# First group of an attention and softplus-layer kernel: keys pooled by TensorE, softplus ahead of weight conversions

## The chip, the cores and the metric

The kernel runs on one core of a Trainium2 chip. Its engines work side by side, each through its own list of instructions in a fixed order: TensorE (PE; weight loads are shown as PEld), VectorE (DVE), ScalarE (ACT), GpSimd (POOL), and SyncE (SP), which here only issues DMAs. The metric is the device time of one execution in microseconds (us), less is better.

## The reference

```python
# attention, 64 heads (8 batches x 8), 576 tokens, 64 wide; keys and values pooled by 8
k_p = k.reshape(B, H, 72, 8, D).mean(axis=3)
v_p = v.reshape(B, H, 72, 8, D).mean(axis=3)
scores = 1/8 * q @ k_p^T
scores -= max(scores); attn = exp(scores); attn /= sum(attn) + 1e-9
x = (attn @ v_p)                       # as 4608 tokens x 512
# softplus layer, 512 -> 2048 -> 512
h = x @ w_in
g = max(h, 0) + log1p(exp(-abs(h)))
x = g @ w_out
# gated experts: a skip score and 8 gate logits for each token, one expert of 8 (512 -> 1024 -> 512)
```

## The kernel before

The tokens go through attention and the softplus layer in nine groups of 512. A group's attention is four *units*, one for each pair of heads; the four units of group g+1 are made while group g is in the softplus layer. Group 0 has no such cover: its four units (`unit0`) run first, with on-chip room that later holds weights.

A unit pools the keys, copies the pooled keys of two heads into a block-diagonal tile `kbd` (two copies on ACT), multiplies (`s`), takes maximum, difference, exponential, sum and reciprocal (`shares`), transposes the shares (on TensorE in group 0, by DVE and 12 DMAs later), pools and transposes v into `vp`, and multiplies again (`o`). Every product that needs full precision is done with a high and a low half: `xh` is `o` rounded (ACT), `xl` the rest (DVE). Unit 3 of a group writes the last quarter of `xh` and `xl`.

The softplus layer runs in 16 chunks of 128 hidden columns. `p1(g, c)` has 12 matmuls into a bank `h`; four quarters of the input, three matmuls each. The softplus is Abs, Exp, Ln on ACT (L718 to L720), the sum `a` on DVE (L721), the rounded half `gh` on ACT (L723), the rest `gl` on DVE (L725). There are two banks `h`, and L721 reads a bank last, so p1 of a chunk waits for L721 of the chunk two before. `p2(g, c)` adds 12 matmuls into four banks `y`, two chunks behind p1. When the last chunk of a group is through, `finish` copies the four banks to `rows` (ACT, L113) and makes 36 gating products of 128x512 with them on DVE (L119).

The weights of this layer arrive as pairs of 32-bit words that hold both halves of the bits, and have to be converted during group 0 (`load_weights`): two unpacks on ACT (`unpack`), two joins on DVE (`join`), the rounded half on ACT, the rest on DVE. The first four 128-row blocks go in halves of 512 columns, six of them ahead of group 0 through three buffers `raw`, the others in pairs of whole blocks of 1024 columns. Each of these steps is one turn of a generator, and the loops that make group 0 call it between chunks (`weights(n)`); `ready(c)` says how many turns chunk c needs.

The order of the instructions on each engine is made when the kernel is built: the code emits them in the order of its loops, and a scheduler moves them by its own estimate of when each could run. In the trace the rows of each engine come in the order so made, so an instruction that waits holds up those behind it on its engine.

Of the kernel before, what the change touches and what calls it, by code (L numbers as in the profile page):

```python
# [9 lines left out]
F32 = mybir.dt.float32  # L10
F32R = mybir.dt.float32r
BF16 = mybir.dt.bfloat16
I32 = mybir.dt.int32
# [7 lines left out]
P = 128  # L21
# [8 lines left out]
XW = 520  # L30
BIG = float(1 << 20)
LAG = 2


@with_exitstack
def tile_kernel(ctx, tc, qT, kT, vT, wbits, w9, w1, w2, out):
# [383 lines left out]
    with ExitStack() as ph:  # L420
# [6 lines left out]
        ep = ph.enter_context(tc.tile_pool(name="ep", bufs=1))  # L427
        ps_a = ph.enter_context(tc.tile_pool(name="ps_a", bufs=2, space=PSUM))
        ps_h = ph.enter_context(tc.tile_pool(name="ps_h", bufs=2, space=PSUM))
        ps_y = ph.enter_context(tc.tile_pool(name="ps_y", bufs=1, space=PSUM))  # L430

        kbd = []
        for i in range(2):
# [21 lines left out]
            return pool.tile([P, n], F32, tag=tag, name=tag)  # L455

        EARLY = 4
        STEPS = 6 * EARLY + 6 * (8 - EARLY // 2)
# [4 lines left out]
        def load_weights():  # L463


            bits = wbits.bitcast(I32)

            def unpack(lo, hi):
                nc.scalar.activation(out=hi.bitcast(F32), in_=hi.bitcast(F32), func=AF.Copy,
                                     scale=2.0 ** -112)  # L470
                nc.scalar.activation(out=lo, in_=lo.bitcast(U32), func=AF.Copy, scale=7.49 * 2.0 ** -32)

            def join(v, lo, hi):
                nc.vector.scalar_tensor_tensor(out=v, in0=hi, scalar=3, in1=lo,
                                               op0=ALU.logical_shift_left, op1=ALU.bitwise_or)
# [3 lines left out]
            def half(c, j, first):  # L479
                wh, wl = (wt[c // 2][:, c % 2, i, j * 512:(j + 1) * 512] for i in range(2))  # L480
                if first:
                    raw = room("raw", 1024, True).bitcast(I32).rearrange("p (a b) -> p a b", b=2)
                else:
                    raw = scratch.tile([P, 512, 2], I32, tag="raw", name="raw")
                nc.sync.dma_start(out=raw.rearrange("p a b -> p (a b)"),
                                  in_=bits[c * P:(c + 1) * P, j * 1024:(j + 1) * 1024])
                lo, hi = raw[:, :, 0], raw[:, :, 1]
                unpack(lo, hi)
# [10 lines left out]
            for c in range(EARLY):  # L499
                for j in range(2 if c >= LAG else 1):  # L500
                    yield from half(c, j, True)
            for i in range(EARLY // 2, 8):
                raw = wtile(i, f"raw{i}", 2, 1024, 2, dtype=I32)
                for j in range(2):
                    c = 2 * i + j
                    nc.sync.dma_start(out=raw[:, j].rearrange("p a b -> p (a b)"), in_=bits[c * P:(c + 1) * P, :])
                vs = []
                for j in range(2):
                    lo, hi = raw[:, j, :, 0], raw[:, j, :, 1]
                    unpack(lo, hi)  # L510
                    yield
                    v = scratch.tile([P, 1024], I32, tag="raw", name="v")
                    join(v, lo, hi)
                    vs.append(v.bitcast(F32))
                    yield
                wt.append(wtile(i, f"wt{i}", 2, 2, 1024, dtype=F32R))
                for j in range(2):
                    wh, wl = wt[i][:, j, 0], wt[i][:, j, 1]
                    nc.scalar.activation(out=wh, in_=vs[j], func=AF.Copy)
                    nc.vector.tensor_tensor(out=wl, in0=vs[j], in1=wh.bitcast(F32), op=ALU.subtract)  # L520
                    yield
            for c in range(LAG):
                yield from half(c, 1, False)

        pooled = {}
        count = [0]
        def keys(u, k, kv):
            if u not in pooled:
                kp = pp.tile([P, SP], F32, tag="kp", name="kp")
                nc.vector.tensor_reduce(kp, k.rearrange("p (s w) -> p s w", w=8), AX.X, ALU.add)  # L530
                v = kv()
                nc.sync.dma_start(out=v, in_=vT[u])
                pooled[u] = (kp, v, None)
            kp = pooled[u][0]
# [4 lines left out]
            return kb  # L539

        def shares(e, sm, rc):
            nc.scalar.activation(out=e, in_=e, func=AF.Exp, scale=1.0 / 64)
# [32 lines left out]
        def unit0(hp, us, xh, xl):  # L575
# [3 lines left out]
            nc.sync.dma_start(out=q, in_=qT[u, :, r0:r0 + rn])  # L579
            yield  # L580
            yield
            banks = [ps_y.tile([P, 512], F32, tag=f"y{hp % 2 * 2 + i}", name="s") for i in range(2)]
            kb = keys(u, k, lambda: room("kv", 576, True))
            for t in range(T):
                nc.tensor.matmul(banks[t // 3][:, t % 3 * 144:(t % 3 + 1) * 144],
                                 lhsT=q[:, t * P:(t + 1) * P], rhs=kb, start=True, stop=True)
# [3 lines left out]
            for b, (i, j) in enumerate(((0, 3), (3, 4))):  # L590
                s3 = banks[b][:, :(j - i) * 144].rearrange("p (a k) -> p a k", k=SP)
                m = mx[:, 2 * i:2 * j]
                nc.vector.tensor_reduce(m, s3, AX.X, ALU.max)
                nc.vector.tensor_tensor(out=e[:, 2 * i:2 * j], in0=s3, op=ALU.subtract,
                                        in1=m.unsqueeze(2).to_broadcast([P, 2 * (j - i), SP]))
            shares(e, sm, rc)
            yield
            yield
            kp, v, _ = pooled[u]
            v8 = v.rearrange("p (s w) -> p w s", w=8)  # L600
            pv = ps_h.tile([P, 512], F32, tag="h", name="pv")
            for w in range(8):
                nc.tensor.matmul(pv[:SP, :P], lhsT=v8[:, w], rhs=ident, start=w == 0, stop=w == 7)
# [103 lines left out]
        def p1(g, c):  # L707
# [9 lines left out]
            a = ap.tile([P, G], F32, tag="a", name="a")  # L717
            nc.scalar.activation(out=a, in_=h, func=AF.Abs)  # L718
            nc.scalar.activation(out=a, in_=a, func=AF.Exp, scale=-1.0)
            nc.scalar.activation(out=a, in_=a, func=AF.Ln, bias=1.0)  # L720
            nc.vector.scalar_tensor_tensor(out=a, in0=h, scalar=0.0, in1=a, op0=ALU.max, op1=ALU.add)  # L721
            gh = gp.tile([P, G], F32R, tag="gh", name="gh")
            nc.scalar.activation(out=gh, in_=a, func=AF.Copy)  # L723
            gl = gp.tile([P, G], F32R, tag="gl", name="gl")
            nc.vector.tensor_tensor(out=gl, in0=a, in1=gh.bitcast(F32), op=ALU.subtract)  # L725
            return gh, gl

        def p2(g, c, gh, gl):
# [13 lines left out]

        def ready(c):
            if c < EARLY:
                return 3 * (2 * c - min(c, LAG)) + 3
            return 3 * (2 * EARLY - LAG) + 6 * ((c - EARLY) // 2) + 6
# [264 lines left out]
```

## Time and profile before

| | us |
|---|---|
| median of 3 runs (lowest to highest) | 1370.47 (1370.27 to 1371.11) |
| profiled execution | 1378.22 |
| its span, first to last instruction | 1376.5 |
| TensorE busy | 1338.4 (97%) |
| VectorE busy | 847.6 (62%) |
| ScalarE busy | 594.6 (43%) |
| GpSimd busy | 309.6 (22%) |
| mean granted TensorE clock | 0.994 of full |

TensorE is busy nearly throughout, and shares over the whole span say little of the first 150 us, where the other engines have their fullest stretch. Windows of the span, the order in time of single engines and the list of waits show that part.

### The profile page before, as it was taken

The numbers are of one execution on the slowest core, as the hardware profiler recorded it, in microseconds if no ns is written. First come the engines' busy times: TensorE is split into PE (matmuls) and PEld (weight loads), VectorE is DVE, ScalarE is ACT, GpSimd is POOL, SyncE is SP. The second block draws the span as 40 slices with busy tenths as digits, with TensorE's granted clock in tenths as the row PEclk, the third lists the DMA queues.
The fourth block names the chain that finished last, engine by engine and source line by source line (L and its number), as shares of the span: only waits on it lengthen the run. The fifth ranks groups of instructions, "written<-read, shape, count | busy, mean of one in ns | idle before, by whom it ended". The sixth has DMA issues, their size and how long they took to land. (4 is left out here: it accounts for less than half of the span.)

```text
span 1376.5 us, 21364 instructions
## 1 busy us (share of the span) xinstructions
PE 1338.4 (97%) x7030; PEld 1114.9 (81%) x7030; DVE 847.6 (62%) x1951; ACT 594.6 (43%) x1076; POOL 309.6 (22%) x374
## 2 busy tenths in 40 slices
PE   6899999999999999999999999999999999999986
PEld 5667877777878778788778778888989898889886
DVE  7997794783974974965956847545645332325254
ACT  6985544544545545455455445541111121114142
POOL 2000012111121121030030120343424243323233
PEclk9999999999999999999999999999999999999998
DMA  8633343241241340431421301513323122225272
GB/s 283 260 115 90 86 136 75 59 130 48 76 125 35 80 129 26 112 106 31 118 70 33 106 13 47 192 39 92 96 70 100 57 76 67 81 61 169 64 269 80
DMA packets 149599, 134.16 MB, mean 97 GB/s; under 512 B 100789, under 2 KB 116789, under 8 KB 146912
## 3 DMA queue, kind: packets, MB, share of 16 engines
q1 hardware_dynamic: 131744, 95.51, 24.0%
q0 software_dynamic: 17728, 37.13, 8.5%
q8 instruction: 59, 0.97, 0.3%
q14 instruction: 68, 0.56, 0.1%
HBM read 166.67 MB, written 29.67 MB: 143 GB/s over the span
## 5 line engine op out<-in xcount | busy, mean ns | idle before, releaser
L715 PE MATMUL h<-xh,wt 128*128 128x512 f32 x1152 | 381.9, 393 | 3.4 <-DVE a L721 3.1
L715 PEld LDWEIGHTS h<-xh,wt 128*128 128x128 f32 x1152 | 217.6, 189 | 51.2 <-DVE a L721 4.9
L894 PE MATMUL h<-xt,w1h 128*128 128x256 f32 x1280 | 229.1, 282 | 4.2 <-ACT w1h L404 1.7
L736 PE MATMUL y<-wt,gh 128*128 128x512 f32 x576 | 233.2, 405 | 0.0
L119 DVE CUSTOM_DVE_ANT_0 junk<-rows,w9b 128x512 bf16<-128x512 f32 x324 | 223.0, 688 | 8.3 <-ACT rows L113 3.2
L715 PE MATMUL h<-xl,wt 128*128 128x512 f32 x576 | 225.7, 392 | 0.0
L737 PE MATMUL y<-wt,gh 128*128 128x512 f32 x576 | 225.4, 391 | 0.0
L738 PE MATMUL y<-wt,gl 128*128 128x512 f32 x576 | 224.7, 390 | 0.0
L894 PEld LDWEIGHTS h<-xt,w1h 128*128 128x128 f32 x1280 | 197.7, 189 | 9.2 <-issue 4.8
L894 PE MATMUL h<-xt,w1l 128*128 128x256 f32 x640 | 180.4, 282 | 3.8 <-issue 2.4
L898 ACT ACTIVATE hs<-h 128x512 fp32r<-128x512 f32 x80 | 47.6, 598 | 307.5 <-PE h L894 170.1
L718 ACT ACTIVATE a<-h 128x512 f32<-128x512 f32 x144 | 85.9, 597 | 184.1 <-PE h L715 172.4
L721 DVE SCALAR_TENSOR_TENSOR a<-h,a 128x512 f32<-128x512 f32 x144 | 98.5, 684 | 101.0 <-ACT a L720 100.4
L723 ACT ACTIVATE gh<-a 128x512 fp32r<-128x512 f32 x144 | 90.8, 630 | 158.5 <-DVE a L721 152.9
L736 PEld LDWEIGHTS y<-wt,gh 128*128 128x128 f32 x576 | 108.1, 188 | 36.5 <-ACT a L718 8.3
L715 PEld LDWEIGHTS h<-xl,wt 128*128 128x128 f32 x576 | 109.0, 189 | 22.9 <-issue 0.7
L738 PEld LDWEIGHTS y<-wt,gl 128*128 128x128 f32 x576 | 108.1, 188 | 23.7 <-DVE gl L725 0.4
L725 DVE TENSOR_TENSOR gl<-a,gh 128x512 fp32r<-128x512 f32 x144 | 99.2, 689 | 42.0 <-ACT gh L723 39.4
L894 PEld LDWEIGHTS h<-xt,w1l 128*128 128x128 f32 x640 | 122.7, 192 | 2.8 <-issue 1.0
L737 PEld LDWEIGHTS y<-wt,gh 128*128 128x128 f32 x576 | 108.3, 188 | 20.1 <-issue 0.4
L920 PE MATMUL y<-w2h,hs 128*128 128x512 f32 x304 | 118.4, 390 | 0.3 <-issue 0.3
L919 PE MATMUL y<-w2l,hs 128*128 128x512 f32 x304 | 118.4, 389 | 0.2 <-issue 0.2
(197 smaller groups left out, 1728.0 us busy)
## 6 DMA issues: line engine op xcount, KB each, us to landing
w9b<-w SPq DMA_DIRECT2D x81, 256.0 KB
raw<-wbits SPq DMA_DIRECT2D x12, 1024.0 KB
x2d<-rows SPq DMA_DIRECT2D x36, 260.0 KB
et<-q SPq DMA_DIRECT2D x256, 32.0 KB
kv<-kT SPq DMA_DIRECT2D x28, 288.0 KB
kv<-vT SPq DMA_DIRECT2D x28, 288.0 KB
xm<-misc SPq DMA_DIRECT2D x160, 32.0 KB
misc<-misc SPq DMA_DIRECT2D x144, 32.0 KB
```

The costliest lines, as they stand in the source:

```text
L119: nc.vector.tensor_tensor_reduce(out=ws["junk"], in0=rows[t][:, :D], in1=w9b[e], scale=1.0, scalar=0.0, op0=ALU.mult, op1=ALU.add, accum_o ...
L715: nc.tensor.matmul(h, lhsT=l, rhs=r[:, kk, :], start=n == 0, stop=n == 11)
L718: nc.scalar.activation(out=a, in_=h, func=AF.Abs)
L721: nc.vector.scalar_tensor_tensor(out=a, in0=h, scalar=0.0, in1=a, op0=ALU.max, op1=ALU.add)
L723: nc.scalar.activation(out=gh, in_=a, func=AF.Copy)
L725: nc.vector.tensor_tensor(out=gl, in0=a, in1=gh.bitcast(F32), op=ALU.subtract)
L736: nc.tensor.matmul(y, lhsT=th, rhs=wh, start=c == 0, stop=False)
L737: nc.tensor.matmul(y, lhsT=th, rhs=wl, start=False, stop=False)
L738: nc.tensor.matmul(y, lhsT=tl, rhs=wh, start=False, stop=c == 15)
L894: nc.tensor.matmul(h[:, f2, :], lhsT=l, rhs=r[:, kk, :], start=n == 0, stop=n == 11)
L919: nc.tensor.matmul(y, lhsT=hh[:, f, js], rhs=ws["w2l"][:, f, :], start=False, stop=False)
L920: nc.tensor.matmul(y, lhsT=hl[:, f, js], rhs=ws["w2h"][:, f, :], start=False, stop=f == 7)
```

## The change

It touches group 0 alone. (1) The keys of a first unit are pooled by eight accumulating matmuls with the identity, `pk`, not by a DVE reduction; `kbd` is copied from that bank, and `kp` is kept by a copy. (2) The scores of a first unit go to a tile of two banks, from a pool with two buffers that is closed before the `y` banks are opened, and the maximum and the difference each take one instruction on both banks. (3) The first two conversion steps of blocks 0 and 1 are ordered behind the first and the second exponential, the pooling matmuls behind the scores of the unit before, and the first loads of weights are issued two halves ahead. (4) In group 0 the softplus is emitted with a higher priority for the scheduler (`AHEAD`). (5) The loop that starts the units calls the conversion less often, and twice a turn once all units are started.

```diff
+AHEAD = 250
-        ps_y = ph.enter_context(tc.tile_pool(name="ps_y", bufs=1, space=PSUM))
+        ps_s_cm = tc.tile_pool(name="ps_s", bufs=2, space=PSUM)
+        ps_s = ps_s_cm.__enter__()
...
+                with ExitStack() as st:
+                    if c < 2 and j == 0:
+                        st.enter_context(tc.issue_after(firsts[c]))
+                    unpack(lo, hi)
...
+            for i in range(2):
+                raws.append(fetch(*early[i]))
+                yield
+            for i, (c, j) in enumerate(early):
+                if i + 2 < len(early):
+                    raws.append(fetch(*early[i + 2]))
+                yield from half(c, j, raws[i])
...
-            banks = [ps_y.tile([P, 512], F32, tag=f"y{hp % 2 * 2 + i}", name="s") for i in range(2)]
-            kb = keys(u, k, lambda: room("kv", 576, True))
+            k8 = k.rearrange("p (s w) -> p w s", w=8)
+            pk = ps_h.tile([P, 512], F32, tag="h", name="pk")[:, :SP]
+            with ExitStack() as after:
+                if scores:
+                    after.enter_context(tc.issue_after(scores[-1]))
+                for w in range(8):
+                    nc.tensor.matmul(pk, lhsT=ident, rhs=k8[:, w], start=w == 0, stop=w == 7)
+            kb = band(pk)
+            kp = pp.tile([P, SP], F32, tag="kp", name="kp")
+            nc.scalar.activation(out=kp, in_=pk, func=AF.Copy)
...
+            nc.vector.tensor_reduce(m, s4, AX.X, ALU.max)
+            nc.vector.tensor_tensor(out=k.rearrange("p (b a k) -> p b a k", b=2, k=SP), in0=s4, op=ALU.subtract,
+                                    in1=m.unsqueeze(3).to_broadcast([P, 2, 4, SP]))
...
+            with ExitStack() as st:
+                if g == 0:
+                    st.enter_context(tc.high_priority(offset=AHEAD))
+                a = ap.tile([P, G], F32, tag="a", name="a")
+                nc.scalar.activation(out=a, in_=h, func=AF.Abs)
...
-            if i:
+            if i % 2:
                 weights(1)
+        feed.tick()
         while feed.units or jobs:
             feed.tick()
-            weights(1)
+            weights(1 if feed.units else 2)
```

On ACT, from the last `xh` of group 0 on. Before (Abs is L718, Exp L719, Ln L720; L469 and L471 are unpacks, L491 and L519 rounded weight halves):

```order
L571 ACTIVATE xh<-o 128x512
L471 ACTIVATE raw_450<-raw_450 128x1024
L469 ACTIVATE raw_450<-raw_450 128x1024
L491 ACTIVATE wt_182<-boot_171 128x512
L718 ACTIVATE a<-h 128x512
L471 ACTIVATE raw_450<-raw_450 128x1024
L719 ACTIVATE a<-a 128x512
L537 ACTIVATE kbd_167<-kp 64x72
L720 ACTIVATE a<-a 128x512
```

Now, at the same place (Abs is L751, Exp L752, Ln L753; L471 and L473 are the unpacks):

```order
L590 ACTIVATE xh<-o 128x512
L471 ACTIVATE raw_518<-raw_518 128x1024
L473 ACTIVATE raw_518<-raw_518 128x1024
L553 ACTIVATE kbd_165<-kp 64x72
L554 ACTIVATE kbd_165<-kp 64x72
L553 ACTIVATE kbd_167<-kp 64x72
L751 ACTIVATE a<-h 128x512
L554 ACTIVATE kbd_167<-kp 64x72
L752 ACTIVATE a<-a 128x512
L471 ACTIVATE raw_518<-raw_518 128x1024
L753 ACTIVATE a<-a 128x512
```

The unpacks are those of a later pair (518 is the next after 473, which took the place of 450). Two of them stand ahead of the first Abs as before, and a third between Exp and Ln instead of between Abs and Exp.

On DVE, where group 1 begins. Before (`xl` of unit 3 is L572, the gating products are L119 and stand further down):

```order
L721 SCALAR_TENSOR_TENSOR a_1290<-h_1277,a_1290 128x512
L725 TENSOR_TENSOR gl_1297<-a_1290,gh_1295 128x512
L553 TENSOR_REDUCE vr_1483<-kv_1381 128x72
L572 SCALAR_TENSOR_TENSOR xl_411<-o_1258,xh_410 128x512
L530 TENSOR_REDUCE kp_1570<-kv_1518 128x72
L721 SCALAR_TENSOR_TENSOR a_1326<-h_1313,a_1326 128x512
```

Now (`xl` of unit 3 is L591, the gating products are L120, each with a short read of its sum; `a_1354` is the softplus sum of the first chunk of group 1):

```order
L120 ISA junk_1131,L_1439<-rows_1446,w9b_1452 128x512
L120 ISA L_1439 128x1
L572 TENSOR_REDUCE vr_1511<-kv_1409 128x72
L120 ISA junk_1131,L_1439<-rows_1440,w9b_1454 128x512
L120 ISA L_1439 128x1
L120 ISA junk_1131,L_1439<-rows_1442,w9b_1454 128x512
L120 ISA L_1439 128x1
L591 SCALAR_TENSOR_TENSOR xl_446<-o_1286,xh_445 128x512
```

Eleven products stand above this piece, and with the three in it 14 come ahead of `xl`. They read `rows`, which are copies of the four `y` banks of group 0.

On TensorE at the same place, now (L588 is the output of unit 3, L665 scores of the next group's first unit, `h_1341` and `h_1380` are the banks of the first two chunks of group 1, `h_1456` is that of the third; `y3_592` belongs to p2 of group 0's last chunk):

```order
L771 MATMUL y3_592<-wt0_181,gl_1325 128x512
L588 MATMUL o_1286<-et_1177,vp_396 64x64 x2
L665 MATMUL s_1402<-kbd0_165,q_1363 128x144
L665 MATMUL s_1402<-kbd1_167,q_1363 128x144
L588 MATMUL o_1286<-et_1177,vp_1216 64x448 x2
L745 MATMUL h_1341<-xh_445,wt0_181 128x512
L745 MATMUL h_1380<-xh_445,wt0_181 128x512
L745 MATMUL h_1341<-xl_446,wt0_181 128x512
L745 MATMUL h_1341<-xh_445,wt0_181 128x512
L745 MATMUL h_1380<-xl_446,wt0_181 128x512
L745 MATMUL h_1380<-xh_445,wt0_181 128x512
L665 MATMUL s_1403<-kbd1_167,q_1363 128x144 x2
```

Before, the output of unit 3 stood inside the last two p2 of group 0 but one, and the first chunk of group 1 was finished ahead of the second. Now all of p2 of group 0 and three quarters of both chunks stand ahead of it, and the last quarter of both behind it.

## Rows read from the trace of the kernel before

**Rows 1.** Windows: stretch, its length, busy time (instructions) by engine, clock, DMA.
```profile
43.77:72.00 28.23, 26.20 (x110) 20.67 (x109) 25.27 (x33) 28.17 (x40) 2.28 (x2) 0.94 0.53 192
72.00:112.00 40.00, 36.90 (x161) 26.57 (x160) 37.57 (x51) 30.39 (x51) 2.82 (x4) 0.96 0.30 93
112.00:154.20 42.20, 41.44 (x193) 31.99 (x192) 24.86 (x42) 24.23 (x46) 2.01 (x4) 1.00 0.43 119
...
165.00:1300.00 1135.00, 1129.34 (x5948) 944.80 (x5947) 679.66 (x1697) 447.54 (x832) 265.18 (x296) 1.00 0.29 82
...
62.50:66.50 4.00, 3.95 (x10) 3.12 (x11) 4.00 (x5) 4.00 (x6) 0.00 (x0) 0.57 0.40 91
```

**Rows 2.** Timeline of TensorE: start, duration, instruction, idle time before it.
```profile
43.77 0.49 PE L715 MATMUL h<-xh,wt 128*128 128x512 f32 x1
...
54.79 0.39 PE L715 MATMUL h<-xh,wt 128*128 128x512 f32 x1
...
57.51 0.39 PE L736 MATMUL y<-wt,gh 128*128 128x512 f32 x1
...
62.55 0.50 PE L715 MATMUL h<-xh,wt 128*128 128x512 f32 x1 [2.03 <-DVE a L721]
...
154.43 0.39 PE L715 MATMUL h<-xh,wt 128*128 128x512 f32 x1
...
337.56 0.39 PE L715 MATMUL h<-xh,wt 128*128 128x512 f32 x1
...
532.58 0.39 PE L715 MATMUL h<-xh,wt 128*128 128x512 f32 x1
```

**Rows 3.** Waits of TensorE, 35 to 130 us: total, times, longest.
```profile
PE h L715 <- DVE a L721: 3.1, 3, 2.0
PE s L635 <- ACT kbd L538: 1.3, 1, 1.3
PE pv L560 <- DVE vr L553: 1.0, 1, 1.0
PE o L569 <- PE s L635: 1.0, 1, 1.0
```

**Rows 4.** Timeline of ACT and DVE, last `xh` and softplus of group 0.
```profile
35.83 0.57 ACT L571 ACTIVATE xh<-o 128x512 fp32r<-128x512 f32 x1
36.31 1.13 ACT L471 ACTIVATE raw<-raw 128x1024 int32<-128x1024 uint32 x1
...
41.17 0.64 ACT L720 ACTIVATE a<-a 128x512 f32<-128x512 f32 x1
...
42.01 0.68 DVE L721 SCALAR_TENSOR_TENSOR a<-h,a 128x512 f32<-128x512 f32 x1
...
72.39 0.62 ACT L720 ACTIVATE a<-a 128x512 f32<-128x512 f32 x1
```

**Rows 5.** Timeline of the start: first pooling, scores, first exponential, later scores.
```profile
3.71 0.75 DVE L530 TENSOR_REDUCE kp<-boot_kv 128x72 f32<-128x576 f32 x1 [2.41 <-DMA boot_kv<-kT]
...
5.09 1.94 PEld L585 LDWEIGHTS s<-kbd,boot 128*128 128x128 f32 x8 [5.09 <-ACT kbd L538]
5.09 2.29 PE L585 MATMUL s<-kbd,boot 128*128 128x144 f32 x8 [5.09 <-ACT kbd L538]
...
10.68 0.67 ACT L542 ACTIVATE boot_kv<-boot_kv 128x576 f32<-128x576 f32 x1
...
22.80 1.15 PE L585 MATMUL s<-kbd,boot 128*128 128x144 f32 x8
```

**Rows 6.** Weight loads by line, 3 to 160 us: busy, mean ns, idle before.
```profile
L603 PEld LDWEIGHTS pv<-ident,boot_kv 128*72 128x72 f32 x48 | 7.6, 234 | 0.0
...
L612 PEld LDWEIGHTS tr<-ident,boot_kv 128*72 128x72 f32 x32 | 3.7, 125 | 7.3 <-POOL boot_kv L546 6.4 <-issue 0.8
```

**Rows 7.** Timeline of group 0's `finish`: a copy of a bank, and gating products.
```profile
155.65 0.61 ACT L113 ACTIVATE rows<-y 128x512 f32<-128x512 f32 x1
...
161.73 0.67 DVE L119 CUSTOM_DVE_ANT_0 junk<-rows,w9b 128x512 bf16<-128x512 f32 x1
...
162.45 0.69 DVE L119 CUSTOM_DVE_ANT_0 junk<-rows,w9b 128x512 bf16<-128x512 f32 x1
```

More of the change, by code (lines that the diff above doesn't have):

```diff
@@ L477, in join, with fetch, half @@
                                                op0=ALU.bitwise_and, op1=ALU.bitwise_or)
-            def half(c, j, first):
+            def fetch(c, j):
+                raw = room("raw", 1024, True)
+                nc.sync.dma_start(out=raw.bitcast(I32), in_=bits[c * P:(c + 1) * P, j * 1024:(j + 1) * 1024])
+                return raw.bitcast(I32).rearrange("p (a b) -> p a b", b=2)
+            def half(c, j, raw):
                 wh, wl = (wt[c // 2][:, c % 2, i, j * 512:(j + 1) * 512] for i in range(2))
-                if first:
-                    raw = room("raw", 1024, True).bitcast(I32).rearrange("p (a b) -> p a b", b=2)
-                else:
+                if raw is None:
                     raw = scratch.tile([P, 512, 2], I32, tag="raw", name="raw")
-                nc.sync.dma_start(out=raw.rearrange("p a b -> p (a b)"),
-                                  in_=bits[c * P:(c + 1) * P, j * 1024:(j + 1) * 1024])
+                    nc.sync.dma_start(out=raw.rearrange("p a b -> p (a b)"),
+                                      in_=bits[c * P:(c + 1) * P, j * 1024:(j + 1) * 1024])
                 lo, hi = raw[:, :, 0], raw[:, :, 1]
-                unpack(lo, hi)
+                with ExitStack() as st:
+                    if c < 2 and j == 0:
+                        st.enter_context(tc.issue_after(firsts[c]))
+                    unpack(lo, hi)
                 yield
@@ L498, in load_weights @@
                 wt.append(wtile(i, f"wt{i}", 2, 2, 1024, dtype=F32R))
-            for c in range(EARLY):
-                for j in range(2 if c >= LAG else 1):
-                    yield from half(c, j, True)
+            early = [(c, j) for c in range(EARLY) for j in range(2 if c >= LAG else 1)]
+            raws = []
+            for i in range(2):
[5 more added lines that the diff above has]
+                yield from half(c, j, raws[i])
             for i in range(EARLY // 2, 8):
@@ L522, in load_weights @@
             for c in range(LAG):
-                yield from half(c, 1, False)
+                yield from half(c, 1, None)
         pooled = {}
@@ L533, in keys, with band @@
                 pooled[u] = (kp, v, None)
-            kp = pooled[u][0]
+            return band(pooled[u][0])
+        def band(kp):
             kb = kbd[count[0] % 2]
@@ L539, in keys @@
             return kb
+        firsts, scores = [], []
         def shares(e, sm, rc):
-            nc.scalar.activation(out=e, in_=e, func=AF.Exp, scale=1.0 / 64)
+            ins = nc.scalar.activation(out=e, in_=e, func=AF.Exp, scale=1.0 / 64)
+            firsts.append(ins.ins)
             nc.vector.tensor_reduce(sm, e, AX.X, ALU.add)
@@ L581, in unit0 @@
             yield
-            banks = [ps_y.tile([P, 512], F32, tag=f"y{hp % 2 * 2 + i}", name="s") for i in range(2)]
-            kb = keys(u, k, lambda: room("kv", 576, True))
+            k8 = k.rearrange("p (s w) -> p w s", w=8)
[8 more added lines that the diff above has]
+            nc.scalar.activation(out=kp, in_=pk, func=AF.Copy)
+            v = room("kv", 576, True)
+            nc.sync.dma_start(out=v, in_=vT[u])
+            s2 = ps_s.tile([P, 1024], F32, tag="s", name="s2")
             for t in range(T):
-                nc.tensor.matmul(banks[t // 3][:, t % 3 * 144:(t % 3 + 1) * 144],
-                                 lhsT=q[:, t * P:(t + 1) * P], rhs=kb, start=True, stop=True)
+                a = t // 2 * 512 + t % 2 * 144
+                ins = nc.tensor.matmul(s2[:, a:a + 144], lhsT=q[:, t * P:(t + 1) * P], rhs=kb, start=True, stop=True)
+            scores.append(ins.ins)
             e = k.rearrange("p (a k) -> p a k", k=SP)
@@ L589, in unit0 @@
             mx, sm, rc = (st[:, i * 8:(i + 1) * 8] for i in range(3))
[L590 to L595, printed above, removed]
+            s4 = s2.rearrange("p (b x) -> p b x", b=2)[:, :, :288].rearrange("p b (a k) -> p b a k", k=SP)
+            m = mx.rearrange("p (b a) -> p b a", b=2)
+            nc.vector.tensor_reduce(m, s4, AX.X, ALU.max)
+            nc.vector.tensor_tensor(out=k.rearrange("p (b a k) -> p b a k", b=2, k=SP), in0=s4, op=ALU.subtract,
+                                    in1=m.unsqueeze(3).to_broadcast([P, 2, 4, SP]))
             shares(e, sm, rc)
@@ L598, in unit0 @@
             yield
-            kp, v, _ = pooled[u]
             v8 = v.rearrange("p (s w) -> p w s", w=8)
             pv = ps_h.tile([P, 512], F32, tag="h", name="pv")
-            for w in range(8):
-                nc.tensor.matmul(pv[:SP, :P], lhsT=v8[:, w], rhs=ident, start=w == 0, stop=w == 7)
+            with tc.issue_after(scores[-1]):
+                for w in range(8):
+                    nc.tensor.matmul(pv[:SP, :P], lhsT=v8[:, w], rhs=ident, start=w == 0, stop=w == 7)
             vp = pp.tile([SP, P], F32, tag="vp", name="vp")
@@ L716, in p1 @@
                     n += 1
[L717 to L725, printed above, removed]
+            with ExitStack() as st:
[3 more added lines that the diff above has]
+                nc.scalar.activation(out=a, in_=h, func=AF.Abs)
+                nc.scalar.activation(out=a, in_=a, func=AF.Exp, scale=-1.0)
+                nc.scalar.activation(out=a, in_=a, func=AF.Ln, bias=1.0)
+                nc.vector.scalar_tensor_tensor(out=a, in0=h, scalar=0.0, in1=a, op0=ALU.max, op1=ALU.add)
+                gh = gp.tile([P, G], F32R, tag="gh", name="gh")
+                nc.scalar.activation(out=gh, in_=a, func=AF.Copy)
+                gl = gp.tile([P, G], F32R, tag="gl", name="gl")
+                nc.vector.tensor_tensor(out=gl, in0=a, in1=gh.bitcast(F32), op=ALU.subtract)
             return gh, gl
```

8 lines of the change are left out of this document (5 added, 3 removed).

## The prediction

> **What bounds the kernel now.** I read the page's busy shares first: TensorE is busy for 97% of the span, so the end moves only where TensorE waits or runs at its lower clock. The windows show where that is [rows 1]: from 43.77 to 154.2 us TensorE has gaps and its clock falls to 0.94 and 0.96 on average, while ScalarE (ACT) is busy for all of the stretch up to 72 and VectorE (DVE) for nearly all of 72 to 112. After 165 us TensorE is busy for 1129.34 of 1135.00 us: nothing is to be won there.
>
> I call the 12 matmuls of one chunk of the first layer p1(n), those of the second p2(n); n counts on through the groups of 16, so p1(16) opens group 1. In a dense stretch p1 takes 57.51 - 54.79 = 2.72 us, and two whole later groups take 532.58 - 337.56 = 195.02 us, so 97.5 us for 16 p1, 16 p2 and the next group's attention [rows 2]. The same content between the starts of p1(2) and p1(18) took 154.43 - 43.77 = 110.7 us [rows 2]. So 13.2 us were lost there, and this is what the change can win. TensorE's waits name the causes: 3.1 us for the softplus sum of line 721, 1.3, 1.0 and 1.0 us for steps of the attention [rows 3]. Behind the longest, of 2.03 us [rows 2], the clock was 0.57 on average for 4 us [rows 1], which cost another 0.43 x 4 = 1.7 us.
>
> **The softplus ahead of conversions.** ACT's listed order shows how far the conversions let it past. Back-to-back rows start about 0.1 us closer than they last (35.83 to 36.31 for one of 0.57) [rows 4]; so I count 0.48 for Abs, 0.52 for Exp, Ln and the rounding, 1.04 for a 1024-wide unpack, 0.95 for a 1024-wide rounding. From the start of the last xh to the end of the first Ln the new list has 5.9 us of work; before it took 35.83 to 41.81, 6.0 us [rows 4]. Nothing is won on the first softplus: two unpacks still stand ahead of its Abs, one between its Exp and Ln. But the next five come sooner: from the first Ln to the sixth the list has 24.3 us, where before the sixth ended 73.0 - 41.8 = 31.2 us behind the first [rows 4]. TensorE wants a chunk each 97.5/16 = 6.1 us, five in 30.5, so from the second on the softplus is ahead of it. The conversions stay in time: the last full pair is rounded 32.8 us of list behind the sixth Ln, and p1(14), which reads it, comes seven chunks, 42.7 us, behind p1(7), which that Ln lets start. I take back the 13.2 us but leave 2.5: 1.5 because the copies into kbd for the second unit's scores stand behind the sixth Exp, 1.0 for small waits. Bounds: 0.5, and the 8.9 us that idle time (2.0 + 3.1 + 0.8) and clock (3.0) cost before in these windows [rows 1].
>
> **The start.** Before, DVE pooled the keys in 0.75 us from 3.71, and scores ran at 5.09 [rows 5]. Now eight accumulating matmuls do it. In the trace one fp32 matmul shows as two instructions: a unit's four score matmuls are eight, 2.29 us at 5.09 and 1.15 us at 22.80; early weight loads of 128x128 take 1.94/8 = 0.243 us [rows 5], later half that. So pooling is 16 x 0.243 = 3.9 us, to 7.6; two copies 0.5; scores 2.29, to 10.5; the second pooling 2.1 if the faster rate holds by then (3.9 if not), to 12.6. On ACT the second unit's copies stand ahead of the first exponential, which so starts at 13.4 against 10.68 [rows 5]; the first conversions wait behind it and don't fill the gap. From there to the last xh ACT's list has 23.8 us, against 19.1 before (conversions drawn forward, and the kp copies). Laid out row by row, with DVE and TensorE beside it, I find 3.2 us of waits in it, 1.3 of them for the third pooling, which stands behind a v pooling on TensorE (before there were 6.1): 13.4 + 23.8 + 3.2 = 40.4 against 35.83 [rows 4], 4.6 us late. Before, the bank for p1(2) was free at 42.69 and score matmuls held it until 43.77 [rows 2, 4], 1.1 us that hide part of it, and the list is 0.1 shorter: p1(2) starts 3.4 us later. Bounds: 6.3 with before's waits; -3 if TensorE has the faster rate from its first pooling on (first exponential at 10.3). DVE loses four reductions of 0.75 us [rows 5] and one of two short ones in each pair on the scores; while it waits for scores that shortens no path, so I cost it and the double bank at nothing.
>
> The pooling reads keys in steps of eight elements. The same step on the stationary side, in the v pooling, gave 128x72 loads of 0.234 us on average, against 0.125 for unstrided ones of that shape [rows 6]. The Trainium skill ("SBUF — State Buffer", section "Door 1: The DMA port swizzle") says that consecutive reads must share a 16-byte line to run at full rate, and that each crossing to another line pays. By the rows, 72 columns hide behind a weight load of 0.243 and the sum stands; by that rule, with the moving side at half rate, an early pooling would take what scores of 144 columns take, 16 x 0.286 = 4.6 us, and the sum would be 0.7 us later. No run here has shown that step on the moving side.
>
> **The second group.** Here the change adds a wait. Before, on DVE, the last part of group 1's input (xl of the fourth unit) stood ahead of group 0's gating products (line 119). Now 14 of them stand ahead of it, and TensorE has p2(15) ahead of that unit's output matmuls. Let E be the end of p2(15). Its first bank is done at E - 2.0 and a copy takes 0.6 [rows 7], so the first product starts at E - 1.3; each takes 0.73 (161.73 to 162.45) [rows 7], 14 take 10.2; a max (0.4) and a v reduction (0.7) stand in between, so xl ends at E + 10.6. What TensorE has without it is over by E + 3. Then the rest of p1(16) and p1(17), two Abs, two Exp and an Ln (0.6 each) and the sum (0.7) [rows 4] pass before a bank is free for p1(18): E + 15.0 at the higher clock, 15.8 at the lower. Without the wait p1(18) would start at E + 3.5 (output 1.3, scores and pooling 0.85, six matmuls 1.36). So 11.5 to 12.3 us are lost, and behind the stall the clock should fall as at 62.55, up to 1.7 more [rows 1]. Bounds 11.5 and 14.0; I take 12.9. One v pooling and a score, done early, give 0.4 back.
>
> **Sum.** -13.2 + 2.5 + 3.4 + 12.9 - 0.4 = +5.2 us at p1(18). Behind it the listed orders are alike and TensorE is full, so it stays to the end. The profiled execution took 1378.2 us, 1.7 of them around its span, 7.7 over the median of the runs; the same shift gives 1383.4 there, and 1370.5 + 5.2 = 1375.7 for the median. About 0.2%, 2.7 us, is what can be told from no change.
>
> **Rivals.**
> - The start is not late. For it: TensorE works from 3.7 us on without the long idle stretch of before, so the faster rate may come sooner. Against: at 5.09 it ran at half that [rows 5]. With -3 for the start, 0.5 left over and 11.5 at the second group: -13.2 - 3 + 0.5 + 11.5 - 0.4 = -4.6, 1365.9 us. It decides once the first exponential starts before about 11 us.
> - The start costs nothing, the rest is as forecast: +1.8, 1372.3 us, no change. That needs the waits on ACT gone from the list.
> - ACT, full until 72 us [rows 1], never gets ahead, because its rows wait for DVE and TensorE in the new order; half of the 13.2 us stays, 4.1 more than forecast: 1379.8 us. Against: its list is 7 us shorter up to the sixth Ln.
> - The priority does nothing on the chip and all 13.2 stay: +15.9, 1386.4 us. The list speaks against it.
>
> **Chances.** Forecast 0.45, start not late 0.23, no cost at the start 0.22, ACT never ahead 0.08, nothing 0.02. The forecast, the third and fourth rival are slower by over 0.2% (0.55), the first faster (0.23), the second within (0.22). The range, 1366.5 to 1381, reaches from near the first rival to just past the third; the forecast's own is 1373.5 to 1379.
>
> **What would show it.** In the changed profile: pooling of about 3.9 us from 3.7 and a first exponential near 13; p1(2) near 47; hardly a wait for the softplus sum between 50 and 135; a TensorE gap of some 7 us between about 146 and 154 that ends with xl, and a lower clock behind it; p1(18) near 159.5. A first exponential at or before 11 us, or no such gap, makes the forecast wrong.

## The result, and the profile after

The changed kernel takes 1382.26 us (median of 4 runs, 1380.80 to 1383.16) against 1370.37 (4 runs, 1369.67 to 1371.11): ratio 1.0086, 95% interval 1.0068 to 1.0103. It is 11.9 us slower. Forecast were 5.2 us and a range up to 1381: the direction is right, the size is not.

Windows of the changed kernel, with the cuts of [rows 1] moved to its own p1(2) and stall: stretch, length, busy time (instructions) of PE, PEld, DVE, ACT, POOL, granted clock, DMA share, GB/s.
```profile
47.07:72.00 24.93, 24.13 (x105) 19.11 (x105) 23.62 (x31) 24.84 (x40) 1.23 (x2) 1.00 0.42 147
72.00:112.00 40.00, 39.57 (x183) 30.10 (x182) 36.90 (x51) 32.59 (x52) 2.76 (x4) 1.00 0.29 94
112.00:145.00 33.00, 32.68 (x150) 25.43 (x149) 20.42 (x32) 17.96 (x36) 2.29 (x4) 1.00 0.42 117
145.00:165.00 20.00, 11.64 (x35) 7.13 (x34) 18.14 (x47) 8.32 (x19) 0.26 (x1) 0.58 0.44 118
165.00:1300.00 1135.00, 1133.60 (x5975) 949.60 (x5974) 675.17 (x1683) 451.42 (x837) 268.03 (x296) 1.00 0.29 82
```
In the first group TensorE has lost most of its gaps (1.5 us are left of 5.9) and its clock stays at 1.00 (0.94 and 0.96 in [rows 1]). Instead there is a stall from 145 to 165 us: 11.64 us busy of 20, at a mean clock of 0.58.

TensorE's waits from 35 to 176 us (total, times, longest) stand against [rows 3]:
```profile
PE o L588 <- DMA et<-q: 3.0, 1, 3.0
PE h L745 <- DVE xl L591: 2.3, 1, 2.3
PE s L665 <- ACT kbd L554: 1.5, 3, 0.8
...
PE h L745 <- DVE a L754: 0.2, 1, 0.2
```
The softplus sum, 3.1 us before, is down to 0.2. The two longest waits are new, and both belong to the last unit of group 1: its transposed shares `et`, which DMAs bring, and its `xl`. TensorE's order in time shows them behind p2(15):
```profile
146.18 0.34 PE L588 MATMUL o<-et,vp 72*64 72x64 f32 x4 [0.62 <-ACT rows L114]
146.44 0.76 PE L665 MATMUL s<-kbd,q 128*128 128x144 f32 x4
150.24 1.76 PE L588 MATMUL o<-et,vp 72*64 72x448 f32 x4 [3.04 <-DMA et<-q]
152.69 1.22 PE L745 MATMUL h<-xh,wt 128*128 128x512 f32 x2 [0.69 <-ACT xh L590]
156.19 0.79 PE L745 MATMUL h<-xl,wt 128*128 128x512 f32 x1 [2.29 <-DVE xl L591]
...
161.86 0.80 PE L745 MATMUL h<-xh,wt 128*128 128x512 f32 x1
```
p2(15) ended at 145.56; p1(18) is the last row, 16.3 us behind. VectorE did run 14 gating products ahead of `xl`; these are the first, the fourteenth and `xl`:
```profile
144.19 0.69 DVE L120 CUSTOM_DVE_ANT_0 junk<-rows,w9b 128x512 bf16<-128x512 f32 x1 [2.89 <-ACT rows L114]
...
154.84 0.69 DVE L120 CUSTOM_DVE_ANT_0 junk<-rows,w9b 128x512 bf16<-128x512 f32 x1
...
155.45 0.69 DVE L591 SCALAR_TENSOR_TENSOR xl<-o,xh 128x512 fp32r<-128x512 f32 x1
```
SP issued the twelve DMAs of this `et` from 140.73 to 148.93, just behind the start of p1(17) at 140.64:
```profile
140.73 8.20 SPq L689 DMA_DIRECT2D et<-q  x12
```
In the kernel before (profiled again below as e5) they were over at 140.97, as p1(16) started (140.83):
```profile
132.18 8.79 SPq L659 DMA_DIRECT2D et<-q  x12
```

**Both kernels in one set.** The kernel before took 1379 us (median) in every later set, against 1370 in the first. Its first profiled execution, 1378.22, agrees with the later ones. So only ratios to the kernel before of the same set are compared, and both kernels were profiled again in one set: the kernel before as e5 (1377.59, span 1375.9), the changed one as e6 (median 1391.07, ratio 1.0087, 1.0071 to 1.0103; span 1387.9). First weight loads of p1(2), p1(16) and p1(18), and the last weight load of the layer's last p1 (2.5 us behind its first), of e5 and then of e6:
```profile
43.65 0.19 PEld L715 LDWEIGHTS h<-xh,wt 128*128 128x128 f32 x1
...
140.83 0.19 PEld L715 LDWEIGHTS h<-xh,wt 128*128 128x128 f32 x1
...
153.85 0.19 PEld L715 LDWEIGHTS h<-xh,wt 128*128 128x128 f32 x1
...
907.37 0.19 PEld L715 LDWEIGHTS h<-xh,wt 128*128 128x128 f32 x1
```
```profile
50.04 0.19 PEld L745 LDWEIGHTS h<-xh,wt 128*128 128x128 f32 x1 [0.52 <-DVE a L754]
...
137.18 0.19 PEld L745 LDWEIGHTS h<-xh,wt 128*128 128x128 f32 x1
...
164.55 0.19 PEld L745 LDWEIGHTS h<-xh,wt 128*128 128x128 f32 x1
...
917.66 0.19 PEld L745 LDWEIGHTS h<-xh,wt 128*128 128x128 f32 x1
```
The differences add up: start +6.4; p1(2) to p1(16) 87.1 against 97.2, -10.0; p1(16) to p1(18) 27.4 against 13.0, +14.4; p1(18) to that last load -0.4; behind it 470.2 against 468.5 to the end of the span, +1.7. Sum 12.0 us, and the profiled spans differ by 12.0. These are one execution of each kernel; no profile of the kernel before belongs to the runs of 1370 us, so the 11.9 us of the result itself can't be split in the same way.

### The profile page after: what moved, and what is told of

Same layout as the page of the kernel before. It is cut to its first block, busy times and chain, and to the rows that moved or that the text cites. A ratio compares the mean times of both kernels' runs of the same rounds, so it can differ in the third digit from the quotient of the medians.

```text
span 1379.0 us, 21489 instructions
## 1 busy us (share of the span) xinstructions
PE 1347.6 (98%) x7094; PEld 1124.1 (82%) x7094; DVE 843.5 (61%) x1939; ACT 594.2 (43%) x1080; POOL 309.8 (22%) x374
## 5 line engine op out<-in xcount | busy, mean ns | idle before, releaser
L120 DVE CUSTOM_DVE_ANT_0 junk<-rows,w9b 128x512 bf16<-128x512 f32 x324 | 222.3, 686 | 11.5 <-ACT rows L114 6.1
L751 ACT ACTIVATE a<-h 128x512 f32<-128x512 f32 x144 | 85.8, 596 | 180.3 <-PE h L745 177.6
L958 DVE SCALAR_TENSOR_TENSOR ys<-y,xg 128x512 f32<-128x512 f32 x38 | 28.5, 751 | 148.0 <-PE y L956 148.0
```

The source lines that it names most:

```text
L120: nc.vector.tensor_tensor_reduce(out=ws["junk"], in0=rows[t][:, :D], in1=w9b[e], scale=1.0, scalar=0.0, op0=ALU.mult, op1=ALU.add, accum_o ...
```

## The experiments

Each has a short diff, abridged here, against the kernel named. The columns are the starts of p1(2), p1(16), p1(18) and of p1(32), which opens group 2, and the time from there to the end of the span (us, first weight loads).

| run | ratio (95%) | p1(2) | p1(16) | p1(18) | p1(32) | rest |
|---|---|---|---|---|---|---|
| e5 before again | one run | 43.65 | 140.83 | 153.85 | 238.74 | 1137.1 |
| changed, first set | 1.0086 (1.0068-1.0103) | 47.07 | 134.25 | 161.79 | 247.95 | 1131.1 |
| e6 changed again | 1.0087 (1.0071-1.0103) | 50.04 | 137.18 | 164.55 | 249.03 | 1138.9 |
| e1 products behind | 1.0052 (1.0037-1.0067) | 50.04 | 137.01 | 161.71 | 246.51 | 1138.6 |
| e2 units early | 0.9997 (0.9984-1.0011) | 49.28 | 138.18 | 151.19 | 236.11 | 1140.9 |
| e3 priority alone | 1.0064 (1.0048-1.0079) | 44.90 | 130.58 | 161.84 | 247.59 | 1137.7 |
| e4 no priority | 1.0090 (1.0071-1.0109) | 49.08 | 151.32 | 163.20 | 249.16 | 1141.1 |
| e7 early, keys on DVE | 0.9939 (0.9921-0.9956) | 41.80 | 131.33 | 145.39 | 229.84 | 1139.7 |
| e8 before + priority, early | 0.9949 (0.9934-0.9964) | 43.29 | 132.78 | 145.79 | 232.21 | 1138.2 |
| e9 output late, et early | 1.0020 (1.0005-1.0034) | 50.24 | 138.59 | 156.45 | 242.54 | 1142.9 |
| e10 e2, four matmuls ahead | 0.9991 (0.9978-1.0004) | 49.99 | 138.89 | 151.89 | 237.12 | 1142.5 |
| e11 e7, six ahead | 0.9951 (0.9933-0.9969) | 44.30 | 132.51 | 145.51 | 230.41 | 1142.5 |
| e12 e7, conversions free | 0.9951 (0.9934-0.9969) | 44.87 | 136.03 | 149.70 | 234.63 | 1138.3 |
| e13 e2, six ahead | 0.9980 (0.9964-0.9996) | 49.34 | 138.16 | 151.16 | 236.24 | 1138.4 |

The rest varies by up to 5.7 us among the runs e1 to e13, and 1131 us in the first profile of the changed kernel, though the orders there are alike. p1(2) itself moved by 3.0 us between the two profiles of the changed kernel. So the profiles tell edits apart by the times from p1(2) to p1(32), and the ratios to some 2 us.

**e1.** Changed kernel; first product of group 0 behind `xl` of the last unit:
```
+ with tc.issue_after(last_xl):     # in finish(0), first product only
      nc.vector.tensor_tensor_reduce(out=ws["junk"], ...)
```


> The changed kernel, but the first of group 0's gating products on VectorE is queued behind the last unit's xl of group 1, so none of the 14 stands ahead of it; TensorE's order up to group 1's end is the same. If the products alone hold group 1 up (the prediction's term), xl comes at the end of p2(15) plus 3 us, the rest of p1(16) follows at once, and the run falls by 11 to 14 us, to 1368-1371 us. The rival: in the profile of the changed kernel the output of that unit waited until 150.24 us for the DMAs of et, and xl could not have been ready before about 153.3 us instead of 156.06; then only 2.8 us and a shorter half-clock stretch come back, 3 to 4.5 us, to 1378-1379.5 us, and TensorE still waits about 3 us for et near 147-150.

Measured 1.0052, 4.8 us below the changed kernel's 1.0087. From p1(2) to p1(32) it takes 196.5 us, e6 199.0: 2.5 us back. TensorE of e1:
```profile
152.99 1.76 PE L591 MATMUL o<-et,vp 72*64 72x448 f32 x4 [3.04 <-DMA et<-q]
155.43 1.22 PE L749 MATMUL h<-xh,wt 128*128 128x512 f32 x2 [0.69 <-ACT xh L593]
156.45 0.63 PE L749 MATMUL h<-xl,wt 128*128 128x512 f32 x1
...
161.74 0.50 PE L749 MATMUL h<-xh,wt 128*128 128x512 f32 x1
```
The wait for `xl` is gone, the one for `et` stays. The rival (3 to 4.5 us back) holds, though the profile gives less and the ratio a little more: the products, which the prediction made the whole stall, are its smaller part.

**e2.** Changed kernel; units of group 1 fed sooner:
```
- feed.start(units_of(g + 1), 6)
+ feed.start(units_of(g + 1), 6 if g else 4)
```


> The changed kernel, but the units of group 1 are fed every 4 ticks instead of every 6, so that the last one is issued six ticks (three chunks) sooner: in the new order its output matmuls stand ahead of p2(14) and no gating product stands ahead of its xl. Both theories of the stall at group 1's start (products, late et) take it away: p1(18) about 3.5 us behind the end of p2(15) instead of 16.2 us, a clock that stays at 1.00, in all 13 to 15 us less than the changed kernel: 1367 to 1369.5 us. Then the start (+3.4) and the first group (-10.3) together make it a little faster than the kernel before (by 1 to 3 us). If what made the changed kernel slow lies elsewhere (at the start or behind the softplus layer), it stays above 1375.

The stall is gone: p1(16) to p1(18) takes 13.0 us, as in e5, and p1(18) follows p2(15)'s last matmul at once:
```profile
151.18 0.39 PE L771 MATMUL y<-wt,gl 128*128 128x512 f32 x1
151.41 0.39 PE L745 MATMUL h<-xh,wt 128*128 128x512 f32 x1
```
Against e6 12.2 us come back between p1(2) and p1(32) (14.4 at the stall, less 1.8 in a group that now holds more attention work, less 0.4 behind p1(18)); by the ratios 12.4 us. That is a little under what was said (13 to 15). That it would beat the kernel before is not shown: p1(32) is 2.6 us sooner, the ratio shows no difference.

**e3.** Kernel before with `high_priority(offset=250)` around the softplus of group 0 and nothing else.

> The kernel before with the high priority of group 0's softplus as the only edit: keys still pooled by VectorE, scores in single banks. In its order the last unit's output of group 1 stands behind p2(15) and 6 gating products ahead of its xl. The first group should win back 10 to 11 us from p1(2) to p1(16). If the products set the second-group wait, 6 of them cost 8 x 0.73 = 5.8 us less than 14, so 1370.4 - 10.7 + 7 = 1366 to 1368 us. If the late output and et set it, the wait is nearly as long as in the changed kernel, 12 to 14 us: 1371 to 1374 us.

p1(2) to p1(16) fell from 97.2 to 85.7 us, and p1(16) to p1(18) rose to 31.3: a stall no shorter than with 14 products, with 6 (p1(18) starts 17.9 us behind the end of p2(15), 16.3 in the changed kernel). TensorE waits for `et` twice:
```profile
143.53 0.39 PE L742 MATMUL y<-wt,gl 128*128 128x512 f32 x1
146.48 0.34 PE L570 MATMUL o<-et,vp 72*64 72x64 f32 x4 [2.56 <-DMA et<-q]
...
150.82 1.76 PE L570 MATMUL o<-et,vp 72*64 72x448 f32 x4 [3.56 <-DMA et<-q]
...
161.85 0.79 PE L716 MATMUL h<-xh,wt 128*128 128x512 f32 x1
```
So the priority alone brings the stall. The run is 7.9 us slower than the kernel before, 4 us and more beyond either theory. By p1(32) it is 8.8 us late: 1.3 at p1(2), -11.5 in the first group, +18.2 at the stall, +0.8 behind it. The late output holds against the products, but I had priced it too low.

**e4.** Changed kernel without the high priority.

> The changed kernel without the high priority of group 0's softplus; pooling by TensorE, double banks and the order of the conversions stay. In its order no gating product stands ahead of the last unit's xl and the output stands ahead of p2(14). By the prediction's terms the start stays 3.4 us late, nothing of the first group's 13.2 us is won, and the second-group wait is gone: 1370.4 + 3.4 = 1373.8 us (1372 to 1376). If the start costs nothing, 1370.4; if the pooling and conversions cost more than the start, above 1377.

No stall (p1(16) to p1(18) 11.9 us), but 12.5 us slower than before, where 3.4 were expected. At p1(2) it is 5.4 late, and p1(2) to p1(16) takes 102.2 us, 5.1 more than in e5 and 15.1 more than in e6: in the new order TensorE waits once for a v pooling and once for a copy into kbd, 4.3 and 3.8 us:
```profile
PE pv L579 <- DVE vr L572: 4.3, 1, 4.3
PE s L665 <- ACT kbd L554: 3.8, 1, 3.8
```
In the first group the priority is worth more here (15.1 us) than in the kernel before (11.5, e3), as the rest of the change made that group worse. In the whole time it is worth nothing as it stands: e4 is at 1.0090 and e6 at 1.0087, for the 15.1 us won in the first group are lost again at the stall (27.4 us from p1(16) to p1(18) against 11.9).

**e5, e6.** Both kernels unchanged, in one set.

> The kernel before, profiled beside the others of this set. If what is left behind the softplus layer between the profiled executions (TensorE there waits up to 1.2 us at a time for nothing the profile shows: 4.4 us in all in the profile of before, none in that of after) is a matter of the execution and not of the kernel, this profile shows such waits too, 4 to 7 us in the last 470 us, and the last p1 of the layer starts at 907 to 909.5 us. If the kernel before has none of them beside the others, the changed kernel costs something there.

> The changed kernel, timed and profiled again beside the kernel before. If the result holds on any run, it is 8.9 us (what its last p1 of the layer was late in the first pair of profiles) to 11.9 us (the medians) slower than the kernel before, ratio 1.0065 to 1.0086; its last p1 starts 8 to 10 us behind that of the kernel before profiled in this set. If the layer decides all, the ratio is at the low end.

The waits that the profile shows no cause for, behind the layer, are a matter of the execution: TensorE has 4.7 us of them in e5 and 6.2 in e6, none in the first profile of the changed kernel. e6's last p1 is 10.3 us behind e5's, a little more than was said. And the start of e6 is 3.0 us later than in that first profile. Start of e6 on TensorE:
```profile
3.89 3.66 PE L607 MATMUL pk<-boot_kv,ident 128*128 128x72 f32 x16 [3.89 <-DMA boot_kv<-kT]
8.11 2.29 PE L616 MATMUL s<-kbd,boot 128*128 128x144 f32 x8 [0.56 <-ACT kbd L554]
10.20 3.52 PE L607 MATMUL pk<-boot_kv,ident 128*128 128x72 f32 x16
14.28 2.29 PE L616 MATMUL s<-kbd,boot 128*128 128x144 f32 x8 [0.56 <-ACT kbd L554]
16.36 3.49 PE L633 MATMUL pv<-ident,boot_kv 128*72 128x128 f32 x16
```
and of the first profile of the changed kernel:
```profile
10.05 2.92 PE L607 MATMUL pk<-boot_kv,ident 128*128 128x72 f32 x16
13.54 1.25 PE L616 MATMUL s<-kbd,boot 128*128 128x144 f32 x8 [0.56 <-ACT kbd L554]
14.62 2.31 PE L633 MATMUL pv<-ident,boot_kv 128*72 128x128 f32 x16
```
The same instructions, but TensorE reached its faster rate later in e6: the traces' first record of the full clock is at 11.77 us in the first profile and at 19.59 in e6. ScalarE waited 0.37 us for the first v pooling in the first profile, and 2.62 in e6:
```profile
19.89 0.27 ACT L635 ACTIVATE vp<-pv 72x128 f32<-72x128 f32 x1 [2.62 <-PE pv L633]
```
The prediction's "2.1 if the faster rate holds by then (3.9 if not)" was decided the wrong way.

**e7.** e2 with the keys of group 0 pooled by VectorE:
```
- with ExitStack() as after:          # behind the scores of the unit before
-     for w in range(8): nc.tensor.matmul(pk, lhsT=ident, rhs=k8[:, w], ...)
- kb = band(pk)
- nc.scalar.activation(out=kp, in_=pk, func=AF.Copy)
+ nc.vector.tensor_reduce(kp, k.rearrange(...), AX.X, ALU.add)
+ kb = band(kp)
```


> The kernel with the units of group 1 fed every 4 ticks, and the keys of group 0 pooled by VectorE again instead of TensorE; double banks, the place of the first conversions and the softplus priority stay. If the pooling on TensorE makes the start late (the prediction's 3.4 us), p1(2) starts 3 to 4 us sooner than with it and the run is 3 to 4 us faster than the run of units fed early (whose ratio to the kernel before was 0.9997), ratio 0.997 to 0.9975. If the start is late for the conversions put behind the first exponentials, or the score banks, nothing comes back (0.9990 to 1.0005).

p1(2) is 7.5 us sooner than in e2, the run 8 us faster by the ratios: twice what was expected, and faster than both kernels. The first exponential (ScalarE) starts at 9.02 us, 14.38 in e6:
```profile
9.02 0.68 ACT L560 ACTIVATE boot_kv<-boot_kv 128x576 f32<-128x576 f32 x1 [1.45 <-DVE boot_kv L617]
```
So TensorE's pooling, with the edge behind the scores and the copy on ScalarE that came with it, made the start late, by more than the change as a whole shows: without it p1(2) stands 1.9 us sooner than in the kernel before, one profile each.

**e8.** Kernel before with two edits, e3's priority and e2's feed.

> The kernel before with two edits only: high priority for group 0's softplus, and the units of group 1 fed every 4 ticks. If the priority wins back the first group's lost time and the stall of the second group came only from the late unit, p1(2) starts as in the kernel before (35.6 to 37 us for p1(0)), the layer ends 9 to 13 us sooner, and the run is 9 to 12 us faster: ratio 0.991 to 0.9935. If feeding the units early costs the first group as much as the stall did (more attention work on ScalarE and VectorE while both are full), 2 to 5 us are left: 0.9965 to 0.9985.

7.0 us faster than the kernel before, between the two cases; p1(32) is 6.5 us sooner. The start is unchanged, p1(2) to p1(16) takes 89.5 us (97.2 before), the stall is absent. The interval overlaps that of e7 (0.9921 to 0.9956), so the priority and the early feed are enough for the gain; that the double score banks, the place of the first conversions or the changed loop, which e7 has beyond them, add anything is not shown.

**e9.** e2 with the last unit's output at low priority, so that it stands behind p2(15) again:
```
+ with tc.high_priority(offset=-250):   # hp == 3, group 1
      output(us, et..., hp, xh, xl)
```


> The kernel with the units of group 1 fed every 4 ticks, but the output of the last unit of that group at low priority: TensorE's order has it behind p2(15) again, as in the changed kernel, while its scores, softmax and et come as early as in the run of units fed early; 5 gating products then stand ahead of its xl. If the place behind p2(15) is all that costs, the stall is as long as in the changed kernel: 1.008 to 1.009 times the kernel before. If it was et that came late, hardly anything is lost against the run of units fed early: 0.9997 to 1.0005. From the rows: output 0.6 us behind the end of p2(15), xl some 3.2 us behind it with 5 products, then six matmuls, two softplus starts, p1(18) about 8 us behind the end of p2(15), of which 3.5 us is work that stood earlier; so 4.5 to 6 us lost: 1.003 to 1.004.

p1(2) to p1(32) takes 192.3 us, 5.5 more than e2; by the ratio 3.2 us more (1.0020, where 1.003 to 1.004 was said). p1(18) starts 8 us behind p2(15) (156.48 against 148.5), as worked out. With e1 the stall comes apart, against e2's 186.8 us: 5.5 us for the output's place with 5 products (e9), 9.6 when `et` is late too and no product stands ahead (e1), 12.2 with 14 products (e6).

**e10, e13.** e2 with matmuls of a zero tile ahead of the first pooling, four and six:
```
+ for _ in range(4):      # e13: 6
+     nc.tensor.matmul(warm[:, :144], lhsT=kbd[0][:, :P], rhs=kbd[0], start=True, stop=True)
```


> The run of units fed early (ratio 0.9997) with four more fp32 score-shaped matmuls of a zero tile on TensorE ahead of the first pooling, from about 1.4 us to 3.8 us, where it idled; nothing reads them and the order of all else is the same. If pooling on TensorE is dear because its first instructions run at half the later rate, and the rate rises with work done before, the second pooling falls from 3.52 to 2.3-2.9 us, the v pooling from 2.76-3.49 to 2.31 us, the first exponential comes at 12 to 13.5 us instead of 14.4, and the run is 2 to 5 us faster: 0.9960 to 0.9983. If the rate does not follow the work before, or the matmuls hold the pooling up, the ratio stays at 0.9990 to 1.0005.

> The run of units fed early with keys pooled by TensorE (ratio 0.9997), with six score-shaped matmuls of a zero tile ahead of the first pooling instead of four, until 4.5 us; nothing reads them. If the low rate is what makes the pooling dear and six are enough to raise the rate as in the run with keys on VectorE, the first pooling takes 2.3 us instead of 3.66, the second too, the first exponential comes at 11 to 12 us instead of 14.4, p1(2) at 45.5 to 47 us instead of 49.3-50.0, and the run is 3 to 4.5 us faster: 0.9965 to 0.998. If the pooling matmuls themselves run at the low rate whatever stands ahead, p1(2) is at 50 to 50.6 us and the ratio 0.999 to 1.0007.

e13 on TensorE:
```profile
1.20 3.25 PE L441 MATMUL warm<-kbd 128*128 128x144 f32 x12 [1.20 <-DVE kbd L437]
4.24 3.53 PE L610 MATMUL pk<-boot_kv,ident 128*128 128x72 f32 x16
8.33 2.29 PE L619 MATMUL s<-kbd,boot 128*128 128x144 f32 x8 [0.56 <-ACT kbd L557]
10.41 3.53 PE L610 MATMUL pk<-boot_kv,ident 128*128 128x72 f32 x16
```
Neither helps: the poolings keep 3.5 us and p1(2) its place, so the low rate through the pooling was not ended by matmuls ahead of it (first record of the full clock at 19.47 us in e10, 17.36 in e13, 17.63 in e2). That e13's interval ends below 1 is not seen in the layer (p1(32) 236.24 against 236.11 in e2); it may be the spread of the rest.

**e11, e12.** e7 with six such matmuls ahead of the scores, and e7 without the edge that queues the first conversions behind the first exponentials (`tc.issue_after(firsts[c])`).

> The run with keys on VectorE and units fed early (ratio 0.9939) with six such matmuls of a zero tile on TensorE ahead of its first scores, from about 1.4 to 4.9 us. If the rate rises earlier, the first scores and the first v pooling (3.37 us there) lose 1 to 3 us, of which ScalarE's list lets 0.5 to 2 us through: 0.9925 to 0.9936. If ScalarE's own list sets the start, no difference: 0.9935 to 0.9943.

> The run with keys on VectorE and units fed early (ratio 0.9939), without the edge that queues the first conversions behind the first exponentials. ScalarE's order then has two conversions ahead of the first exponential, as in the kernel before, which had its first exponential at 10.68 us against 9.02 with the edge. If that edge is what makes the start earlier than in the kernel before (p1(2) at 41.80 against 43.65 us), p1(2) goes back by 1 to 2 us and the ratio is 0.9946 to 0.9954; if the double score banks or the softplus priority do it, it stays at 0.9935 to 0.9943.

e11 reached the faster rate at once (full clock from 4.37 us) and lost it again (half from 7.79 to 18.03), and its order changed (the third unit's scores stand behind the transposes). p1(2) is 2.5 us later, not earlier, and the ratio, 0.9951, lies outside both expected bands, with an interval that overlaps that of e7:
```profile
5.35 1.25 PE L612 MATMUL s<-kbd,boot 128*128 128x144 f32 x8 [0.90 <-ACT kbd L557]
7.73 2.21 PE L612 MATMUL s<-kbd,boot 128*128 128x144 f32 x8 [1.14 <-DMA boot<-qT]
```
In e12 p1(2) goes back by 3.1 us and p1(32) by 4.8. The ratio, 0.9951, lies in the expected band, but its interval overlaps that of e7, and one kernel's p1(2) moved by 3.0 us between executions. That the edge on the conversions is a gain is not shown.

## Why the prediction was right or wrong

- **First group.** Forecast -10.7 from p1(2) to p1(16), measured -10.0 (e6 against e5) and -10.3 in the first pair. Right, and by the mechanism named: the wait for the softplus sum fell from 3.1 to 0.2 us.
- **The start: the step that failed most.** Forecast +3.4, measured +6.4 in e6; the same start gave p1(2) at 50.04 in e1 and 49.28 in e2, so the 47.07 of the first profile, which is what was forecast, is the exception. The term took the faster rate to hold from the second pooling on, and chose 2.1 us for that pooling; it took 3.52, the scores behind it 2.29 and the v pooling 3.49 (1.25 and 2.31 at the faster rate, in the first profile). The first exponential came at 14.38 us instead of 13.4, and the rest of the 3.0 us arose in ScalarE's wait for that v pooling (2.62 us, 0.37 in the first profile). The prediction had the price of the other end (3.9 us, and a bound of 6.3) and took the near one. What the pooling costs in all is larger, 7.5 us (e7 against e2). That the other edits to the start gain the difference, 1.9 us by p1(2), is not shown: it is less than one kernel's p1(2) moved.
- **The second group.** Forecast +12.5, measured +14.4. The size is nearly right, the cause only in part, so the near hit is luck. 14 products do stand ahead of `xl`, and it ended 10.6 us behind p2(15), as laid out; but taking them away gives back 2.5 us (e1; 4.8 by the ratio). "What TensorE has without it is over by E + 3" failed: the output waited for `et` until 150.24, 4.7 us behind p2(15)'s end, and the clock fell to 0.50 (mean of 150 to 162 us). What brings both waits is that the units of group 1 come late against the now faster softplus. The priority does that alone (e3), and feeding them sooner undoes it (e2).
- **Behind the layer.** Forecast nothing, measured +1.7, of which 1.5 are waits without a shown cause that other executions of the same kernel don't have; no cost of the change is shown there.
- **Sum.** 3.0 us of the 6.8 missed lie in the start, 1.9 in the stall, 0.7 in the first group, 1.7 behind the layer, and the change behind p1(18) gives 0.4 back. These add to 6.9; the rest is rounding.
- **Rivals.** "The start is not late" and "costs nothing" fell with the first exponential at 13.64 and 14.38 us. That ScalarE never gets ahead fell with the 10.0 us won in the first group. "The priority does nothing" fell with e4: without it 15.1 us more are spent from p1(2) to p1(16).
- **The strided read.** At the lower rate a pooling took 3.52 to 3.66 us, 0.22 to 0.23 for each of its 16 instructions: a little under the 3.9 of the sum. By the rule of the Trainium skill ("SBUF — State Buffer", "Door 1: The DMA port swizzle"), as the prediction had worked it out, it would have been 4.6. At the faster rate an instruction of the pooling takes 0.143 us (2.29 for 16) and one of the scores, with twice as many unstrided columns, 0.144 (1.15 for 8), so what the stride costs there is not shown.

Open: why TensorE came to its faster rate at different times with the same instructions, and why the kernel before takes 1379 us in four sets, on four chips, and 1370 in another. For the changed kernel, 7.8 of the 8.9 us between the spans of its two profiles lie behind p1(32) (1131.1 and 1138.9 us). The double score banks and the changed loop were not tried alone.

## What to carry to other kernels

When one stage gets faster in a list-scheduled kernel, look at what feeds the next stage on its own clock of ticks: a chain with DMAs in it (here 8 us of `et` issues) does not get faster with it and becomes the wait. A wait that has two causes gives back little when only one is removed, so price each by an experiment that leaves the other. And work put onto an idle engine at the start of a program is to be priced at the rate that the engine has there, at both ends, and the sum of the far ends belongs into the range.

## What the runs showed of the hardware that was not expected

- TensorE got its full clock at different times. The traces' first record of it is at 11.77 us in the first profile of the changed kernel, at 19.59 in e6, from 17.29 to 20.36 in the other runs that pool on TensorE (e1, e2, e4, e9, e10, e13), and at 18.63 and 18.29 in the two profiles of the kernel before. In e6 TensorE had worked since 3.89 with two pauses of 0.56 us. In e11, behind matmuls from 1.20 us on, it came at 4.37 and was lost from 7.79 to 18.03; in e7, without them, at 8.58, and was lost from 12.00 to 18.82.
- Ahead of that first record the granted-clock column counts the clock as full: it reads 1.00 from 10 to 13 us in e6, where the second pooling took 3.52 us instead of 2.29. At the start the durations show the rate, and that column does not.
- The same program's span behind the layer differs by several us among executions, in waits of up to 1.2 us for which the profile shows no cause.
